# A cached-attention decode stack on one core: four edits at its first reads, its MLP weights, its last task and its last block

## The chip, the cores and the metric

The kernel runs on one core of one Trainium2 chip. The metric is device time in microseconds (us), the median of the runs of one program. A core has a matrix engine (PE, with its weight loads as PEld), VectorE (DVE), ScalarE (ACT), GpSimd (POOL), and SyncE (SP), which here only issues DMAs; 16 DMA engines move the data between HBM and SBUF. Each engine executes its own instructions in program order, and engines wait for one another through semaphores.

## The reference

```python
x = A_x                                                   # 8 sequences, 1 token each, D = 512
x = x + attention(layernorm(x), K, V, wq, wo)             # 32 query heads, 8 K/V heads, 8192 cached keys, Dh = 128
x = x + silu(layernorm(x) @ w1) @ w2                      # F = 1792
x = x + attention(layernorm(x), K, V, wq, wo)             # the same caches and weights again
x = x + silu(layernorm(x) @ w1) @ w2
# attention: q = x @ wq;  p = softmax(q K^T / sqrt(128));  o = p V;  o @ wo
# layernorm: (x - mean) / sqrt(var + 1e-5);   all tensors are bf16
```

K and V hold 134 MB each. Both layers read V whole; K is read in both layers except for 20 of the 32 granules of each sequence, which stay in SBUF between the layers. The HBM reads are 465 MB.

## The kernel before

**Tasks and positions.** A task is one (layer, sequence, K/V head); there are 128. A program loop counts positions p, eight to a task; each position emits the steps that are due on the engines. A granule is 512 KB of K or V, a quarter of one head's cache; it fills one of 28 slots of the SBUF tile ARENA. Per task: DVE transposes K in place (L485), PE forms the scores (L551) into PSUM bank SCp, DVE and POOL find the maximum (L562 to L574), ACT exponentiates (L578), PE and ACT transpose the probabilities (L596, L600), and PE multiplies them with V (`emit_pv`, L615), 14 positions (LP) behind the scores.

**A V product and its fold.** A V granule has 16 chunks of 128 keys per partition group. `emit_pv` takes four chunks at a time as 512 columns against 16 probability columns (4 chunks x 4 heads); of the result in the PSUM bank OTp only the blocks in which both chunks agree count. `emit_own` (ACT, L627) takes the first block of 128 columns with a mask (`own_x`), `emit_join` (DVE, L633, three instructions) adds the three others into the same f32 tile `joint`, `emit_fold` (PE, L640) sums the partitions in f32 with the mask `hm`, and `emit_norm` (DVE, L650) divides. All tasks do this alike. `add_heads` then applies wo to that head (L755).

**Loads.** SP issues every DMA, in program order (L376, or L102 where a separate wait precedes it). `plan_loads` fixes the order and the position after which each load's slot is free; `issue_until(p)` issues what is free after position p. At the start come x (8 rows), four K granules, wq, all loads that fit in the empty arena, then `load_rest`: wo in 1 KB rows, w1 in 3.5 KB rows, w2 in 1 KB rows (its rows dealt over partitions as ft*128 + p). After them come the loads that need a slot again. x lands in the tile E (also called P and Xr); PE transposes it with the identity matrix that POOL makes (L414, L417, L849), then comes the first LayerNorm and, when wq is there, the queries.

**Chains.** When a sequence has finished layer 0, its output projection, MLP and layer-1 queries are done one stage per position among the other tasks (`chain_of`). The first such chain starts at position 81.

**The last block.** After the last task the second MLP runs for all 8 sequences at once, with nothing beside it (`last_block`): residual add (L885), mean by a matmul with a constant matrix (L889), centring (`c32`, L894), squares and their sum (L897, L898), variance by an f32 matmul (L900), inverse root by Ln and Exp on ACT and a Newton step on DVE (L903 to L909, the result is `gain`), `xnT = c32 * gain` (L911), w1 in two halves of the hidden units (L919, 28 matmuls each, banks SCp 0 and 1), for each half the silu as exp (ACT, L924), add, reciprocal and product (DVE, L925 to L927, the result is `hsT`), w2 in two halves (L931), residual (L936), transposition (L942), two copies (L946, L948) and the store. `last_constants` (L879, L880) writes the constant matrices into an arena slot that is free by then, at the first position of the last task.

```python
def load_rest():
    dma(sp, wo_sb[:, :, :], A_wo.rearrange("(h p) d -> p h d", p=128), wsem["wo"], writes=["wo"])
    dma(sp, w1_sb[:, :, :], B_w1.rearrange("(kt p) f -> p kt f", p=128), wsem["w1"], writes=["w1"])
    dma(sp, w2_sb[:, :, :], B_w2.rearrange("(ft p) d -> p ft d", p=128), wsem["w2"], writes=["w2"])
```

Of the kernel before, what the change touches and what calls it, by code (L numbers as in the profile page):

```python
# [22 lines left out]
PRE = 10  # L23
LP = 14
EARLY = 4
WO_FROM = 36
NTP = 2
NSCP = 2
# [7 lines left out]
JOIN_AT = 1  # L36
FOLD_AT = 3
XW = 4
PIECES = (2, 2, 4)
NQS = 4  # L40
NAT = 2
CW = 32
SETTLE = 1
HALVES = 2

BF16 = mybir.dt.bfloat16
FP32 = mybir.dt.float32
# [193 lines left out]
def _build(ctx, nc, A_x, A_k_cache, A_v_cache, A_wq, A_wo, B_w1, B_w2, out):  # L241
# [120 lines left out]
    def op(eng, inst_fn, reads=(), writes=()):  # L362
        reads = [res(n) if isinstance(n, str) else n for n in reads]
        writes = [res(n) if isinstance(n, str) else n for n in writes]
        syn.acquire(eng, reads, writes)
        inst = inst_fn()
        tok = syn.mark(inst, eng)
        syn.release(tok, reads, writes)
        return tok

    def dma(eng, out_ap, in_ap, counter, reads=(), writes=()):
        reads = [res(n) if isinstance(n, str) else n for n in reads]
        writes = [res(n) if isinstance(n, str) else n for n in writes]
        syn.acquire(eng, reads, writes)
        tok = counter.next_tok()
        eng.dma_start(out_ap, in_ap).then_inc(counter.sem, 16)  # L376
        syn.release(tok, reads, writes)
        return tok

    def mm_group(steps, reads=(), writes=()):  # L380
        def run():
            inst = None
            for f in steps:
                inst = f()
            return inst
        return op(pe, run, reads, writes)
# [21 lines left out]
    with nc.Block() as block:  # L408

        @block.sync  # L410
        def _(sync_eng):
            dma(sp, Xr[0:B, :], x_in, wsem["x"], writes=["P"])

            op(pool, lambda: pool.memset(ident[:, :], 1.0), writes=["ident"])  # L414
            op(
                pool,
# [35 lines left out]
            def issue_until(pos):  # L452
                while queue and queue[0].after <= pos:
                    issue(queue.pop(0))
# [2 lines left out]
                dma(sp, wq_sb[:, :, :], A_wq.rearrange("(kt p) n -> p kt n", p=128), wsem["wq"], writes=["wq"])  # L457

            def load_rest():
                dma(sp, wo_sb[:, :, :], A_wo.rearrange("(h p) d -> p h d", p=128), wsem["wo"], writes=["wo"])  # L460
                dma(sp, w1_sb[:, :, :], B_w1.rearrange("(kt p) f -> p kt f", p=128), wsem["w1"], writes=["w1"])
                dma(sp, w2_sb[:, :, :], B_w2.rearrange("(ft p) d -> p ft d", p=128), wsem["w2"], writes=["w2"])

            for _n in range(NGRAN):
                issue(queue.pop(0))
            load_wq()
            issue_until(-2)
# [141 lines left out]
            def emit_pv(i):  # L609
                ti = i // GPT  # L610
                b, g, k, _h = where(i)
                slot = v_slot[(b, g, k)]
                ob, pb = ti % 2, ti % NPT
                steps = [
                    lambda t=t: pe.matmul(  # L615
                        OTp[ob][t * QUAD:t * QUAD + USED, :],
                        PT[pb][:, k, t].rearrange("p x r -> p (x r)"),
                        ARENA[:, slot * SLOT + t * KB:slot * SLOT + (t + 1) * KB],
                        start=(k == 0), stop=(k == NGRAN - 1),
                    )  # L620
                    for t in range(NQ)
                ]
                mm_group(steps, reads=[r_half(slot, 0), r_half(slot, 1), f"PT{pb}"], writes=[f"OT{ob}"])

            def emit_own(ti):
                ob = ti % 2
                op(act, lambda: act.activation(joint, OTp[ob][:, 0:DH], ACT.Copy, scale=own_x[:, 0:1]),  # L627
                   reads=[f"OT{ob}", "own_x"], writes=["P"])

            def emit_join(ti):  # L630
                ob = ti % 2
                for x in range(1, XW):
                    op(dve, lambda x=x: dve.scalar_tensor_tensor(  # L633
                        joint, OTp[ob][:, x * DH:(x + 1) * DH], own_x[:, x:x + 1], joint, op0=ALU.mult, op1=ALU.add),
                       reads=[f"OT{ob}", "own_x", "P"], writes=["P"])

            def emit_fold(ti):
                ob = ti % 2
                mm_group([
                    lambda: pe.matmul(OTp[ob][:, 0:REP], joint, hm[:, :], start=True, stop=True)  # L640
                ], reads=["P", "hm"], writes=[f"OT{ob}"])
# [231 lines left out]
            mean_w = spare[:, 0:128]  # L873
            words = spare[:, 128:].bitcast(FP32)
            var_w, c32, q32 = words[:, 0:128], words[:, 128:128 + KT * B], words[:, 160:160 + KT * B]
            part, gain, step_ = words[:, 192:192 + B], words[:, 200:200 + B], words[:, 208:208 + B]

            def last_constants():
                op(dve, lambda: dve.memset(mean_w, 1.0 / D), writes=r_calm + ["mean_w"])  # L879
                op(dve, lambda: dve.memset(var_w, 1.0 / D), reads=r_calm, writes=["var_w"])  # L880

            def last_block():

# [6 lines left out]
                    for k in range(KT)  # L890
# [3 lines left out]
                op(dve, lambda: dve.tensor_tensor(  # L894
                    c3, x1[:, :, :], QSp[:, 0:B].unsqueeze(1).to_broadcast(wide), ALU.subtract),
                   reads=["XT1", "QS"], writes=["c32"])
                op(dve, lambda: dve.tensor_tensor(q32, c32, c32, ALU.mult), reads=["c32"], writes=["q32"])  # L897
                op(dve, lambda: dve.tensor_reduce(part, q3.rearrange("p k b -> p b k"), AX.X, ALU.add),  # L898
                   reads=["q32"], writes=["part"])
                mm_group([lambda: pe.matmul(QSp[:, B:2 * B], var_w, part, start=True, stop=True)],  # L900
                         reads=["var_w", "part"], writes=["QS"])
                var = QSp[:, B:2 * B]
                op(act, lambda: act.activation(gain, var, ACT.Ln, bias=eps[:, 0:1], scale=GUESS ** -2),  # L903
                   reads=["QS", "eps"], writes=["gain"])
# [3 lines left out]
                   reads=["QS", "step_"], writes=["step_"])  # L908
                op(dve, lambda: dve.scalar_tensor_tensor(gain, step_, 3.0 * GUESS ** 2, gain, op0=ALU.subtract, op1=ALU.mult, reverse0=True),  # L909
                   reads=["step_", "gain"], writes=["gain"])  # L910
                op(dve, lambda: dve.tensor_tensor(xnT[:, :, :], c3, gain.unsqueeze(1).to_broadcast(wide), ALU.mult),  # L911
                   reads=["c32", "gain"], writes=["xnT"])

                cut = [FT * j // HALVES for j in range(HALVES + 1)]
                for j, (lo, hi) in enumerate(zip(cut, cut[1:])):
                    n = (hi - lo) * B
                    bank, rb = SCp[j % NSCP], f"SC{j % NSCP}"
                    mm_group([
                        lambda o=o, k=k: pe.matmul(bank[:, (o - lo) * B:(o - lo + 1) * B], w1_sb[:, k, o * 128:(o + 1) * 128], xnT[:, k, :],  # L919
                                                   start=(k == 0), stop=(k == KT - 1))  # L920
                        for o in range(lo, hi) for k in range(KT)
                    ], reads=["w1", "xnT"], writes=[rb])
                    ev, re = E[:, lo * B:hi * B], f"e_{j}"
                    op(act, lambda: act.activation(ev, bank[:, 0:n], ACT.Exp, scale=-1.0), reads=[rb, "P"], writes=[re])  # L924
                    op(dve, lambda: dve.tensor_scalar(ev, ev, 1.0, None, op0=ALU.add), reads=[re], writes=[re])  # L925
                    op(dve, lambda: dve.reciprocal(ev, ev), reads=[re], writes=[re])
                    op(dve, lambda: dve.tensor_tensor(hsT[:, lo * B:hi * B], bank[:, 0:n], ev, ALU.mult),  # L927
                       reads=[rb, re], writes=[f"hs_{j}"])
                for j, (lo, hi) in enumerate(zip(cut, cut[1:])):
                    mm_group([  # L930
                        lambda o=o, k=k: pe.matmul(  # L931
# [8 lines left out]
                for j in range(2):  # L940
# [7 lines left out]
                op(act, lambda: act.copy(Xr[0:B, w:D], SCp[1][0:B, 0:w]),  # L948
                   reads=["SC1"] + [f"e_{j}" for j in range(HALVES)], writes=["P2"])

            chain = []
            chain_b = [None]
            turn = [0]
            last0 = {b: max(task_at[(0, b, g)] for g in range(HKV)) for b in range(B)}
            first1 = {b: min(task_at[(1, b, g)] for g in range(HKV)) * GPT for b in range(B)}
            ntask = len(tasks)

            kept_from = min(g for g, _k in kept)

# [5 lines left out]
            for p in range(NG + LP + GPT + FOLD + 1):  # L965
# [32 lines left out]
                if done >= 0 and done % GPT == 0 and done // GPT < ntask:  # L998
                    tj = done // GPT
                    emit_norm(tj)  # L1000
                    layer, b, _g = tasks[tj]
                    if layer == 0:
                        heads[b].append(_g)
                    elif b == B - 1:
                        heads[B].append(_g)
                    if layer == 0 and tj == last0[b]:
                        assert not chain and turn[0] == b
                        chain.extend([lambda b=b: add_heads(b)] * (HKV - summed[b]) + chain_of(b))
                        chain_b[0] = b
                        turn[0] = b + 1  # L1010
                issue_until(p)
                if p == NG - GPT:
                    last_constants()
# [37 lines left out]
```

## Time and profile before

| | |
|---|---|
| median of 3 runs | 1164.85 us (1164.71 to 1164.93) |
| profiled execution | 1164.56 us |
| its span, first to last instruction | 1162.4 us |
| DVE, PE, ACT, POOL busy | 744.6, 730.0, 322.9, 116.7 us |
| PEld (beside PE) | 351.6 us |
| HBM read | 465.05 MB, 400 GB/s over the span |
| chain of waits, shares of the span | DMA 55%, SP's queue 15%, PE 12%, DVE 10% |

The page is of one profiled execution. Times within the span count from its first instruction. In a timeline line the columns are start, duration, engine, source line, operation, output and inputs, shapes, number of instructions merged, and in brackets how long the engine was idle before and what released it; "SPq" marks the issue of a DMA. In the windows, each line has a stretch of time, its length, busy time and number of instructions of PE, PEld, DVE, ACT and POOL, the granted PE clock, the mean share of the 16 DMA engines and GB/s.

### The profile page before, as it was taken

The page shows a single profiled execution, that of the slowest core. Times are in us where ns is not written, and L with a number is a line of the kernel's source. Part 1 is how long each engine was busy: PE and PEld are TensorE (multiplying, and loading weights), DVE is VectorE, ACT ScalarE, POOL GpSimd, SP SyncE. Part 2 cuts the span into 40 slices and gives each one's busy share as a digit, 9 for nine tenths or more (in the row PEclk, how much of TensorE's full clock was granted, in tenths as well). Part 3 has the DMA queues.
Part 4 walks back from the last instruction along what each step waited for, and adds up shares of the span by engine and source line. Part 5 has one row for each costly group of instructions (what it writes and reads, how often), then busy time and mean ns, then how long its engine had stood idle before and what let it go on. Part 6 is the DMA issues. An engine that isn't in the chain of part 4 may idle for free.

```text
span 1162.4 us, 27108 instructions
## 1 busy us (share of the span) xinstructions
PE 730.0 (63%) x11006; PEld 351.6 (30%) x11006; DVE 744.6 (64%) x1782; ACT 322.9 (28%) x759; POOL 116.7 (10%) x296
## 2 busy tenths in 40 slices
PE   1526677656765576567656676667666676657665
PEld 1212342223322342124222342234222332234233
DVE  3827674776557675767467755777477755767473
ACT  0203224223332233222422233222322232223322
POOL 0000101001110011001100011001100011001110
PEclk9995566555765566555855556555755576555655
DMA  9999999999999999999999999999999999999993
GB/s 369 394 397 411 408 408 414 416 410 402 404 418 413 409 402 417 414 409 402 413 414 413 404 394 416 416 409 407 409 417 411 407 403 419 412 408 403 409 408 159
DMA packets 116572, 466.84 MB, mean 402 GB/s; under 512 B 12240, under 2 KB 18144, under 8 KB 108768
## 3 DMA queue, kind: packets, MB, share of 16 engines
q1 hardware_dynamic: 116448, 465.11, 100.0%
q8 instruction: 87, 1.43, 0.5%
q14 instruction: 37, 0.30, 0.1%
HBM read 465.05 MB, written 0.01 MB: 400 GB/s over the span
## 4 chain that ended last, share of the span: by engine, by line
DMA 55%; SPq 15%; PE 12%; DVE 10%; issue 4%; ACT 3%; POOL 1%; DVEq 0%; ACTq 0%
DMA arena<-in_A_v_cache_dram 55%; SPq L376 15%; PE OTp L615 4%; DVE E L633 3%; DVE arena L485 2%; PE SCp L551 2%; PE MISC L737 2%; PE OTp L640 2%; PE TPp L596 1%; ACT E L578 1%; DVE row L562 1%; ACT PT L600 1%; POOL tops L567 1%; ACT E L627 1%; DVE row L574 1%
## 5 line engine op out<-in xcount | busy, mean ns | idle before, releaser
L485 DVE STREAM_TRANSPOSE arena<-arena 128x1024 int32<-128x1024 int32 x352 | 434.3, 1236 | 152.1 <-DMA arena<-in_A_k_cache_dram 151.7
L615 PE MATMUL OTp<-arena,PT 128*16 128x512 bf16 x2048 | 282.0, 553 | 295.7 <-DMA arena<-in_A_v_cache_dram 274.7
L578 ACT ACTIVATE E<-SCp,row 128x512 bf16<-128x512 f32 x128 | 181.9, 1421 | 596.0 <-DVE row L574 585.5
L551 PE MATMUL SCp<-arena,QB 128*16 128x128 bf16 (+2 forms) x4608 | 254.5, 366 | 20.5 <-DVE arena L485 14.0
L633 DVE SCALAR_TENSOR_TENSOR E<-OTp,row,E 128x128 f32<-128x128 f32 x384 | 131.4, 342 | 116.2 <-ACT E L627 105.0
L615 PEld LDWEIGHTS OTp<-arena,PT 128*16 128x16 bf16 x2048 | 50.3, 91 | 435.8 <-DMA arena<-in_A_v_cache_dram 401.1
L551 PEld LDWEIGHTS SCp<-arena,QB 128*16 128x16 bf16 x4608 | 107.3, 110 | 103.9 <-issue 52.5
L567 POOL PARTITION_ALL_REDUCE tops<-top x128 | 47.5, 371 | 582.2 <-DVE top L564 435.6
L596 PE MATMUL TPp<-ident,E 128*128 128x128 bf16 x512 | 71.7, 288 | 33.7 <-ACT E L578 32.6
L587 POOL PARTITION_ALL_REDUCE ssa<-ssm x128 | 55.8, 436 | 359.9 <-ACT ssm L585 359.9
L600 ACT COPY PT<-TPp 128x256 bf16<-128x256 bf16 x128 | 47.6, 372 | 156.1 <-PE TPp L596 156.1
L640 PE MATMUL OTp<-row,E 128*128 128x4 f32 x256 | 70.2, 345 | 24.4 <-DVE E L633 24.4
L562 DVE TENSOR_REDUCE row<-SCp 128x1 f32<-128x512 f32 x128 | 84.5, 660 | 0.7 <-PE SCp L551 0.7
L640 PEld LDWEIGHTS OTp<-row,E 128*128 128x128 f32 x256 | 59.0, 287 | 85.5 <-DVE E L633 49.9
L596 PEld LDWEIGHTS TPp<-ident,E 128*128 128x128 bf16 x512 | 40.8, 124 | 101.9 <-ACT E L578 72.0
L755 PE MATMUL MISC<-at,wo 128*128 128x32 bf16 x1024 | 37.3, 187 | 18.8 <-DVE row L571 12.7
L627 ACT ACTIVATE E<-OTp,row 128x128 f32<-128x128 f32 x128 | 47.5, 371 | 3.7 <-PE OTp L615 3.7
L737 PE MATMUL MISC<-xnT,wq 128*128 128x32 bf16 (+1 forms) x1152 | 35.6, 186 | 14.1 <-DVE xnT L724 14.1
L737 PEld LDWEIGHTS MISC<-xnT,wq 128*128 128x128 bf16 x1152 | 34.6, 105 | 20.6 <-issue 18.4
L755 PEld LDWEIGHTS MISC<-at,wo 128*128 128x128 bf16 x1024 | 32.9, 105 | 25.4 <-DVE at L650 22.3
L585 ACT ACTIVATE ssm<-row 128x4 f32<-128x4 f32 x128 | 37.9, 296 | 3.8
L525 DVE TENSOR_TENSOR QB<-QSp,row 128x64 bf16<-128x64 f32 x128 | 25.8, 202 | 19.6 <-PE QSp L512 19.5
(94 smaller groups left out, 302.6 us busy)
## 6 DMA issues: line engine op xcount, KB each, us to landing
arena<-in_A_v_cache_dram SPq DMA_DIRECT2D x512, 512.0 KB, 11.0
arena<-in_A_k_cache_dram SPq DMA_DIRECT2D x192, 512.0 KB, 8.3
arena<-in_A_k_cache_dram SPq DMA_DIRECT2D x24, 2048.0 KB, 22.3
arena<-in_A_k_cache_dram SPq DMA_DIRECT2D x32, 1024.0 KB, 19.9
wq<-in_A_wq_dram SPq DMA_DIRECT2D x1, 4096.0 KB, 16.5
wo<-in_A_wo_dram SPq DMA_DIRECT2D x1, 4096.0 KB, 35.0
w<-in_B_w_dram SPq DMA_DIRECT2D x2, 1792.0 KB, 26.5
E<-in_A_x_dram SPq DMA_DIRECT2D x1, 8.0 KB
```

The costliest lines, as they stand in the source:

```text
L376: eng.dma_start(out_ap, in_ap).then_inc(counter.sem, 16)
L485: op(dve, lambda: dve.transpose(words, words), reads=[r_half(slot, 0), r_half(slot, 1)], writes=[r_half(slot, 0), r_half(slot, 1)])
L551: lambda n=n, t=t: pe.matmul(SCp[bank][t * QUAD:t * QUAD + USED, lo * 128:(lo + len(slots)) * 128], QB[qn][:, n, :], keys(t, n), start=(n ...
L562: op(dve, lambda: dve.tensor_reduce(rowmax[:, :], SCp[bank][:, :], AX.X, ALU.max), reads=[f"SC{bank}"], writes=["rowmax"])
L578: op(act, lambda: act.activation(P[:, :].rearrange("p (x j k) -> p k x j", x=CPB, k=NGRAN), SCp[bank][:, :].rearrange("p (k x j) -> p k x ...
L596: lambda c=c: pe.transpose(tpv[:, c, :], P[:, c * 128:(c + 1) * 128], ident[:, :])
L600: op(act, lambda: act.copy(PT[pb][:, :, :, :, :].rearrange("p a t x r -> p x t a r"), tpv.rearrange("p x (t q) -> p x t q", q=QUAD)[:, :, ...
L615: lambda t=t: pe.matmul(OTp[ob][t * QUAD:t * QUAD + USED, :], PT[pb][:, k, t].rearrange("p x r -> p (x r)"), ARENA[:, slot * SLOT + t * KB ...
L633: op(dve, lambda x=x: dve.scalar_tensor_tensor(joint, OTp[ob][:, x * DH:(x + 1) * DH], own_x[:, x:x + 1], joint, op0=ALU.mult, op1=ALU.add ...
L640: lambda: pe.matmul(OTp[ob][:, 0:REP], joint, hm[:, :], start=True, stop=True)
L737: lambda o=o, k=k: pe.matmul(MISC[:, o * n:o * n + w], w_sb[:, k, o * 128:(o + 1) * 128], rhs_of(k).to_broadcast([128, w]) if n == 1 else ...
L755: lambda o=o, h=h: pe.matmul(MISC[:, o * w:(o + 1) * w], wo_sb[:, h, o * 128:(o + 1) * 128], rhs_of(h).to_broadcast([128, w]) if n == 1 el ...
```

## The change

Four edits:

1. The first K granule is issued ahead of x.
2. `load_rest` loads w1 first, into the memory of w2 (`undealt`), then wo. At the end of position 30, `deal_w1` has ACT copy w1 from there to its own place in four copies, one for each 128 input rows, with its columns reordered (hidden unit p*14 + ft goes to tile ft, place p), and SP then loads w2 in rows of 14 KB, partition p holding hidden units p*14 to p*14+13. The DMA of w2 waits for the four copies.
3. For the last task alone, each V granule is multiplied in two turns of 256 columns and 8 probability columns (XL = 2), both added into the same 256 columns of PSUM; ACT copies these 256 columns, and the fold is two f32 matmuls with the masks in `own_last` in place of the mask and the three additions. `last_constants` makes `own_last`.
4. In the last block w1 is applied to the centred rows (`xnT` is a copy of `c32`, on ACT) and its result scaled by `gain` (two DVE multiplications, into `scaled`). Two of the 14 column tiles of w1 (AHEAD) stand ahead of the variance matmul on PE, the others behind it. Both exponentials are emitted before the add, reciprocal and product of either half.

```diff
+DEAL_AT = 30
+XL = 2
+AHEAD = 2
...
-            dma(sp, Xr[0:B, :], x_in, wsem["x"], writes=["P"])
...
             def load_rest():
+                dma(sp, undealt, B_w1.rearrange("(kt p) f -> p kt f", p=128), wsem["w1"], writes=["w2"])
                 dma(sp, wo_sb[:, :, :], A_wo.rearrange("(h p) d -> p h d", p=128), wsem["wo"], writes=["wo"])
-                dma(sp, w1_sb[:, :, :], B_w1.rearrange("(kt p) f -> p kt f", p=128), wsem["w1"], writes=["w1"])
-                dma(sp, w2_sb[:, :, :], B_w2.rearrange("(ft p) d -> p ft d", p=128), wsem["w2"], writes=["w2"])
-
-            for _n in range(NGRAN):
+            undealt = w2_sb[:, :, :].rearrange("p ft d -> p (ft d)").rearrange("p (kt f) -> p kt f", kt=KT)
+            def deal_w1():
+                for k in range(KT):
+                    op(act, lambda k=k: act.copy(w1_sb[:, k, :].rearrange("p (ft q) -> p ft q", ft=FT),
+                                                 undealt[:, k, :].rearrange("p (q ft) -> p ft q", ft=FT)),
+                       reads=["w2"], writes=["w1"])
+                dma(sp, w2_sb[:, :, :], B_w2.rearrange("(p ft) d -> p ft d", p=128), wsem["w2"], writes=["w2"])
+            issue(queue.pop(0))
+            dma(sp, Xr[0:B, :], x_in, wsem["x"], writes=["P"])
+            for _n in range(1, NGRAN):
                 issue(queue.pop(0))
             load_wq()
             issue_until(-2)
             load_rest()
...
+                w = XL if ti == ntask - 1 else XW
                 steps = [
-                    lambda t=t: pe.matmul(
-                        OTp[ob][t * QUAD:t * QUAD + USED, :],
-                        PT[pb][:, k, t].rearrange("p x r -> p (x r)"),
-                        ARENA[:, slot * SLOT + t * KB:slot * SLOT + (t + 1) * KB],
-                        start=(k == 0), stop=(k == NGRAN - 1),
+                    lambda t=t, y=y: pe.matmul(
+                        OTp[ob][t * QUAD:t * QUAD + w * REP, 0:w * DH],
+                        PT[pb][:, k, t, y * w:(y + 1) * w].rearrange("p x r -> p (x r)"),
+                        ARENA[:, slot * SLOT + t * KB + y * w * DH:slot * SLOT + t * KB + (y + 1) * w * DH],
+                        start=(k == 0 and y == 0), stop=(k == NGRAN - 1 and y == CPB // w - 1),
                     )
-                    for t in range(NQ)
+                    for y in range(CPB // w) for t in range(NQ)
...
             def emit_own(ti):
+                if ti == ntask - 1:
+                    op(act, lambda: act.copy(E[:, 0:XL * DH], OTp[ob][:, 0:XL * DH]), reads=[f"OT{ob}"], writes=["P"])
+                    return
...
             def emit_join(ti):
+                if ti == ntask - 1:
+                    return
...
             def emit_fold(ti):
+                if ti == ntask - 1:
+                    mm_group([
+                        lambda x=x: pe.matmul(OTp[ob][:, 0:REP], E[:, x * DH:(x + 1) * DH], own_last[:, x * REP:(x + 1) * REP],
+                                              start=(x == 0), stop=(x == XL - 1))
+                        for x in range(XL)
+                    ], reads=["P", "own_last"], writes=[f"OT{ob}"])
+                    return
...
             def last_constants():
+                op(dve, lambda: dve.tensor_tensor(
+                    own_last.rearrange("p (x r) -> p x r", r=REP), own_x[:, 0:XL].unsqueeze(2).to_broadcast([128, XL, REP]),
+                    hm[:, :].unsqueeze(1).to_broadcast([128, XL, REP]), ALU.mult),
+                   reads=["own_x", "hm"] + r_calm, writes=["own_last"])
...
             def last_block():
+                op(act, lambda: act.copy(xnT[:, :, :], c3), reads=["c32"], writes=["xnT"])
                 op(dve, lambda: dve.tensor_tensor(q32, c32, c32, ALU.mult), reads=["c32"], writes=["q32"])
...
+                rise(0, AHEAD)
                 mm_group([lambda: pe.matmul(QSp[:, B:2 * B], var_w, part, start=True, stop=True)],
                          reads=["var_w", "part"], writes=["QS"])
+                rise(AHEAD, cut[1])
+                for lo, hi in zip(cut[1:], cut[2:]):
+                    rise(lo, hi)
...
-                op(dve, lambda: dve.tensor_tensor(xnT[:, :, :], c3, gain.unsqueeze(1).to_broadcast(wide), ALU.mult),
-                   reads=["c32", "gain"], writes=["xnT"])
...
+                    op(dve, lambda: dve.tensor_tensor(
+                        scaled[j].rearrange("p (o b) -> p o b", b=B), SCp[j][:, 0:n * B].rearrange("p (o b) -> p o b", b=B),
+                        gain.unsqueeze(1).to_broadcast([128, n, B]), ALU.mult),
+                       reads=[f"SC{j}", "gain"], writes=[f"scaled_{j}"])
...
+                if p == DEAL_AT:
+                    deal_w1()
                 issue_until(p)
```

`rise(lo, hi)` issues the w1 matmuls (four for each column tile) of the tiles lo to hi - 1.

More of the change, by code (lines that the diff above doesn't have):

```diff
@@ L459, in load_rest @@
             def load_rest():
+                dma(sp, undealt, B_w1.rearrange("(kt p) f -> p kt f", p=128), wsem["w1"], writes=["w2"])
                 dma(sp, wo_sb[:, :, :], A_wo.rearrange("(h p) d -> p h d", p=128), wsem["wo"], writes=["wo"])
-                dma(sp, w1_sb[:, :, :], B_w1.rearrange("(kt p) f -> p kt f", p=128), wsem["w1"], writes=["w1"])
-                dma(sp, w2_sb[:, :, :], B_w2.rearrange("(ft p) d -> p ft d", p=128), wsem["w2"], writes=["w2"])
-            for _n in range(NGRAN):
+            assert KT * F == FT * D
+            undealt = w2_sb[:, :, :].rearrange("p ft d -> p (ft d)").rearrange("p (kt f) -> p kt f", kt=KT)
[8 more added lines that the diff above has]
+            for _n in range(1, NGRAN):
                 issue(queue.pop(0))
@@ L875, in _ @@
             var_w, c32, q32 = words[:, 0:128], words[:, 128:128 + KT * B], words[:, 160:160 + KT * B]
+            own_last = words[:, 376:376 + XL * REP]
             part, gain, step_ = words[:, 192:192 + B], words[:, 200:200 + B], words[:, 208:208 + B]
@@ L899, in last_block, with rise @@
                    reads=["q32"], writes=["part"])
+                cut = [FT * j // HALVES for j in range(HALVES + 1)]
+                def rise(lo, hi):
+                    j = max(n for n in range(HALVES) if cut[n] <= lo)
+                    mm_group([
+                        lambda o=o, k=k: pe.matmul(SCp[j][:, (o - cut[j]) * B:(o - cut[j] + 1) * B],
+                                                   w1_sb[:, k, o * 128:(o + 1) * 128], xnT[:, k, :],
+                                                   start=(k == 0), stop=(k == KT - 1))
+                        for o in range(lo, hi) for k in range(KT)
+                    ], reads=["w1", "xnT"], writes=[f"SC{j}"])
+                assert HALVES <= NSCP
+                rise(0, AHEAD)
                 mm_group([lambda: pe.matmul(QSp[:, B:2 * B], var_w, part, start=True, stop=True)],
                          reads=["var_w", "part"], writes=["QS"])
+                rise(AHEAD, cut[1])
+                for lo, hi in zip(cut[1:], cut[2:]):
+                    rise(lo, hi)
                 var = QSp[:, B:2 * B]
@@ L910, in last_block @@
                    reads=["step_", "gain"], writes=["gain"])
-                op(dve, lambda: dve.tensor_tensor(xnT[:, :, :], c3, gain.unsqueeze(1).to_broadcast(wide), ALU.mult),
-                   reads=["c32", "gain"], writes=["xnT"])
-                cut = [FT * j // HALVES for j in range(HALVES + 1)]
+                scaled = [words[:, 256 + lo * B:256 + hi * B] for lo, hi in zip(cut, cut[1:])]
                 for j, (lo, hi) in enumerate(zip(cut, cut[1:])):
[L916 to L922, printed above, removed]
+                    n = hi - lo
+                    op(dve, lambda: dve.tensor_tensor(
+                        scaled[j].rearrange("p (o b) -> p o b", b=B), SCp[j][:, 0:n * B].rearrange("p (o b) -> p o b", b=B),
+                        gain.unsqueeze(1).to_broadcast([128, n, B]), ALU.mult),
+                       reads=[f"SC{j}", "gain"], writes=[f"scaled_{j}"])
                     ev, re = E[:, lo * B:hi * B], f"e_{j}"
-                    op(act, lambda: act.activation(ev, bank[:, 0:n], ACT.Exp, scale=-1.0), reads=[rb, "P"], writes=[re])
+                    op(act, lambda: act.activation(ev, scaled[j], ACT.Exp, scale=-1.0), reads=[f"scaled_{j}", "P"], writes=[re])
+                for j, (lo, hi) in enumerate(zip(cut, cut[1:])):
+                    ev, re = E[:, lo * B:hi * B], f"e_{j}"
                     op(dve, lambda: dve.tensor_scalar(ev, ev, 1.0, None, op0=ALU.add), reads=[re], writes=[re])
                     op(dve, lambda: dve.reciprocal(ev, ev), reads=[re], writes=[re])
-                    op(dve, lambda: dve.tensor_tensor(hsT[:, lo * B:hi * B], bank[:, 0:n], ev, ALU.mult),
-                       reads=[rb, re], writes=[f"hs_{j}"])
+                    op(dve, lambda: dve.tensor_tensor(hsT[:, lo * B:hi * B], scaled[j], ev, ALU.mult),
+                       reads=[f"scaled_{j}", re], writes=[f"hs_{j}"])
                 for j, (lo, hi) in enumerate(zip(cut, cut[1:])):
@@ L949, in last_block @@
                    reads=["SC1"] + [f"e_{j}" for j in range(HALVES)], writes=["P2"])
+            ntask = len(tasks)
             chain = []
@@ L955, in _ @@
             first1 = {b: min(task_at[(1, b, g)] for g in range(HKV)) * GPT for b in range(B)}
-            ntask = len(tasks)
             kept_from = min(g for g, _k in kept)
```

## The prediction
> **What bounds the kernel now.** I read the page's slices first, to see which resource is never idle.
>
> ```profile
> DMA  9999999999999999999999999999999999999993
> GB/s 369 394 397 411 408 408 414 416 410 402 404 418 413 409 402 417 414 409 402 413 414 413 404 394 416 416 409 407 409 417 411 407 403 419 412 408 403 409 408 159
> ```
>
> The DMA engines are full in every slice but the last. PE and DVE are busy under two thirds of the time, so work moved on them in the middle is worth nothing. The time is three pieces: the start of the stream, its bytes over its rate, and what is computed after the last bytes. Next I read the first issues in the timeline, and the rate by stretch in the windows (last column GB/s, the one before it the DMA share).
>
> ```profile
> 0.79 0.39 SPq L376 DMA_DIRECT2D E<-in_A_x_dram  x1
> 1.24 1.78 SPq L376 DMA_DIRECT2D arena<-in_A_k_cache_dram  x4
> ```
> ```profile
> 9.00:18.00 9.00, 0.24 (x4) 0.19 (x4) 2.93 (x12) 0.00 (x0) 0.28 (x1) 1.00 1.02 423
> 51.00:60.00 9.00, 0.64 (x8) 0.00 (x0) 4.06 (x8) 0.00 (x0) 0.37 (x1) 1.00 1.10 348
> 67.00:71.00 4.00, 0.00 (x0) 0.00 (x0) 0.00 (x0) 0.00 (x0) 0.00 (x0) 1.00 1.10 356
> 80.00:1140.00 1060.00, 694.02 (x10342) 330.02 (x10334) 699.68 (x1670) 308.29 (x727) 111.15 (x278) 0.58 1.02 410
> ```
>
> K's first transfer is issued 0.45 us after x. The stretches are wq in 8 KB rows (423), wo in 1 KB rows (348), w2 in 1 KB rows (356), and the caches, mostly 4 KB rows (410): 1 KB rows keep the engines just as busy and move a seventh less. Last comes the end: the chain of waits names the last transfer that anything waited for, and the timeline gives the steps behind it.
>
> ```profile
> 1121.70 15.49 DMA arena<-in_A_v_cache_dram
> ```
> ```profile
> 1148.63 0.37 ACT L627 ACTIVATE E<-OTp,row 128x128 f32<-128x128 f32 x1 [3.74 <-PE OTp L615]
> 1149.10 1.12 DVE L633 SCALAR_TENSOR_TENSOR E<-OTp,row,E 128x128 f32<-128x128 f32 x3 [2.14 <-ACT E L627]
> ...
> 1150.28 0.59 PE L640 MATMUL OTp<-row,E 128*128 128x4 f32 x2 [1.70 <-DVE E L633]
> ...
> 1152.38 0.19 DVE L894 TENSOR_TENSOR arena<-XT,QSp 128x32 f32<-128x32 bf16 x1 [0.43 <-PE QSp L889]
> ...
> 1153.10 0.59 PE L900 MATMUL QSp<-arena 128*128 128x8 f32 x2 [0.82 <-DVE arena L898]
> ...
> 1154.94 0.19 DVE L911 TENSOR_TENSOR xnT<-arena 128x32 bf16<-128x32 f32 x1
> ...
> 1155.19 1.66 PE L919 MATMUL SCp<-xnT,w 128*128 128x8 bf16 x56 [1.50 <-DVE xnT L911]
> ...
> 1156.39 0.19 DVE L925 TENSOR_SCALAR E<-E 128x56 f32<-128x56 f32 x1 [1.25 <-ACT E L924]
> ...
> 1158.18 0.22 DVE L927 TENSOR_TENSOR hsT<-SCp,E 128x56 bf16<-128x56 f32 x1
> ```
>
> The chain leaves the DMA at 1137.19 and is compute from there: softmax of the last task, its V product, fold, output projection, last block. The last V transfer is issued at 1132.4 and lands 14.9 later, at 1147.3, just ahead of the product that reads it. So whatever moves all landings earlier moves the end by as much, and the 14 us from there on are a chain in which every step counts.
>
> **The change, part by part.** The profiled execution is 1164.56 us, 1162.4 of span and 2.16 around it; the median of the runs is 1164.85. I work in differences and apply them to the median.
>
> *K first.* K's first issue moves from 1.24 to 0.79: the stream starts 0.45 us earlier. The second K issue stays at 1.65, while the first brings 512 KB, 1.28 us at 410 GB/s, and packets follow an issue by about a microsecond, so the stream doesn't run dry between. x now lands behind K's first granule, which took 3.9 from issue to landing, so at some 5 to 6 us. Its cover is the identity: the transposes of x (L849) wait for POOL's L417, done at 9.38; without that cover the first LayerNorm would start late, but the queries wait for wq at 19.5 anyway. Minus 0.45; bounds 0 and 0.45.
>
> *w2 in 14 KB rows.* 1.835 MB took 1.835/0.352 = 5.2 us at the 1 KB rates (348 and 356). At 410 to 423 they take 4.5 to 4.3. Minus 0.8; bounds 0.5 and 0.9. The page "DMA: Bandwidth & Descriptors" of the Trainium skill (Specifications) puts line rate at 512 B and up, by which 1 KB rows would be full rate already and this term nought; the rows at 348 and 356 say otherwise.
>
> *w1 landed in w2's place and dealt on ACT; w2 behind it.* w1 keeps its 3.5 KB rows, only ahead of wo. wo's issue lands 35.0 after 27.8, at 62.8; behind w1 it comes about 4 us later, 66.9, still ahead of its first use, which was at 77.0. The deal is four ACT copies of 1,792 elements with a read step of 28 bytes. Plain f32 or bf16 copies cost about 0.18 us plus 0.75 ns an element (128x32 0.18, 8x256 0.36), which makes 1.5 us each; the exponential L578, which writes in 8-byte steps, takes 1.42 us for 512, 2.4 ns an element, which makes 4.5. All four: 6 to 18 us. ACT stands idle from 50.1 to 76.9 in the trace of before, waiting for the exponential of task 3, and w1 lands at about 55: the deal ends between 61 and 73. The page "SBUF — State Buffer" (Door 1) of the Trainium skill says a step beyond 16 bytes pays for every access, which speaks for the upper figure. Either way it is hidden or delays the fourth exponential (71 now, since the V of task 2 no longer waits for w2) by 2 us, and the stream doesn't see that. The wait is new on SP's queue: w2 waits for the deal, and behind it stand all loads from position 37 on. By the loads' order, 15 loads (12 V granules and 4 MB of K, 10.5 MB, 25.6 us) lie between wo and w2, so they land by 66.9 + 25.6 = 92.5, and SP, which issues some 15 us ahead, comes to w2 at about 77. The deal is done by then. Cost 0.
>
> *The constants.* One more DVE multiply (0.2 to 0.36, as L525) at the place of L879; the PE waits over a microsecond for V at 1132 and 1137 behind it. Cost 0.
>
> *The last task.* Each of its four granules is 8 matmuls of 256 columns for 4 of 512. L551 runs 16 of 128 columns in the 0.60 us that L615 needs for 4 of 512: cost goes by columns. I take plus 0.05; the upper bound, if a matmul cost the same at 256, is a granule of 1.1 for 0.55, plus 1.7 in all, since the first two have 0.4 of slack before the fold of task 126. Then L627's 0.37 becomes a copy of 256 columns (0.36 by L948, 0.8 by L578's rate), the three L633 (1148.99 to 1150.28 with hops: 1.29) go, and the fold is two pairs of f32 passes: 0.59 plus about 0.50. Minus 1.29, plus 0.07 hop and 0.50: minus 0.7; bounds 0.3 and 0.8.
>
> *The last block.* Now c32 ends at 1152.57. After: ACT's copy to xnT 1152.62 to 1152.80; the first 8 matmuls of w1 (1.66/56 = 0.030 each) 1152.86 to 1153.10. Behind them in PE's queue stands the variance matmul, for which Ln, gain and both scalings wait; its input is ready at 1153.04, so it goes at 1153.12 for 1153.10. The gain is ready at 1154.94 for 1154.91. Meanwhile PE does the other 48, first half by 1154.4, second by 1155.2. The two scalings (0.22 each, as L927) run 1155.0 to 1155.5, the first exponential ends at 1155.51, and the six DVE operations that ran 1156.39 to 1158.40 start at 1155.56 and end at 1157.57. Minus 0.85; bounds 0.5 and 1.0. The w2 half behind it and the rest stay.
>
> Sum: -0.45 - 0.8 + 0.05 - 0.7 - 0.85 = -2.75 us: the profiled run 1161.8, the median 1162.1. A measurement of this kernel can tell about 0.2%, 2.3 us, from no change; the limit is 1162.5, so the forecast is faster by little over it.
>
> **Rivals.** *1 KB rows are no slower in this place:* the w2 term is nought, -1.95, 1162.9. For it: the engines' share was 1.10 in those stretches, so packets overlapped. Against it: two stretches at 350. 0.08. (The 512 B rule of the Trainium skill's DMA page would give this.)
>
> *The last engine.* The stream ends by its slowest DMA engine: in the windows its rate falls 406, 317, 180, 33 GB/s over 1140 to 1148, so engines end up to 4 us apart. Program fetches of 16 KB (87 of them) share these engines, 0.6 us each at 410/16 GB/s; two more on the last engine take 1.3 back: 1163.4. For it: the spread; against it: the program hardly grows. 0.13.
>
> *Matmuls cost by count,* the bound above: +1.7 for 0.05, 1163.75. L551 speaks against it. 0.06.
>
> *The deal holds SP* (the slower side). If the copies take so long that w2 is not issued by about 90, the stream runs dry, and each microsecond beyond is lost. To end 2.3 us slower it must eat 2.75 + 2.3 = 5.1 us, so end at 95: 40 us for four, 10 each, over twice what the slowest row gives. 1168 or so at 10.3 each. That, or a like stall of SP behind it: 0.06.
>
> **The numbers.** Forecast 0.67, rivals 0.08, 0.13, 0.06, 0.06. Faster by over 0.2%: 0.67; within 0.2%, the first three rivals: 0.27; slower: 0.06. The range runs from the good bounds of most terms, -0.45 - 0.9 - 0.8 - 1.0 = -3.15 with an engine's 0.8 more, 1160.9, up to the two middle rivals at 1163.5; it leaves out the deal's stall and the worst matmuls.
>
> **What would show it.** K's issue at 0.79; x after it, L849 still at 9.5. The stretch with w2 at 410 GB/s or more. Four ACT copies between 55 and 73, SP not waiting for them. The last V landing 1.25 earlier, at 1146.0. No L633 after it, four f32 passes in 1.1 us; the w1 matmuls beside Ln and gain, and hs of the second half done 2.75 us ahead of 1158.4. Wrong if SP waits for ACT near 77, if the last landing has not moved, or if the variance matmul starts over 0.3 us after its input.

## The result, and the profile after

The changed kernel takes 1162.26 us (median of 14 runs, 1161.62 to 1163.14); the kernel before takes 1164.64 us over the 14 runs beside them (1164.42 to 1164.93). The ratio is 0.9979, 95% interval 0.9971 to 0.9987: 2.4 us faster, and the interval leaves out no change. The runs of the changed kernel spread three times as far as those of before beside them, 1.5 us for 0.5; in the later series, with 26 to 33 runs, those of the kernel before spread by 1.4 to 1.6 too.

The profiled execution has a span of 1159.9 us, 2.5 less than before. Its end first, in the chain of waits (start, duration, what) and the timeline:

```profile
1121.35 15.10 DMA arena<-in_A_v_cache_dram
```
```profile
1147.91 0.37 ACT L641 COPY E<-OTp 128x256 f32<-128x256 f32 x1 [3.73 <-PE OTp L628]
...
1148.33 1.01 PE L659 MATMUL OTp<-arena,E 128*128 128x4 f32 x4 [0.48 <-ACT E L641]
...
1150.86 0.19 DVE L924 TENSOR_TENSOR arena<-XT,QSp 128x32 f32<-128x32 bf16 x1 [0.43 <-PE QSp L919]
1151.08 0.22 ACT L927 CAST xnT<-arena 128x32 bf16<-128x32 f32 x1 [2.80 <-DVE arena L924]
...
1151.35 0.38 PE L937 MATMUL SCp<-xnT,w 128*128 128x8 bf16 x8 [0.60 <-ACT xnT L927]
...
1151.59 0.57 PE L945 MATMUL QSp<-arena 128*128 128x8 f32 x2
...
1152.02 1.42 PE L937 MATMUL SCp<-xnT,w 128*128 128x8 bf16 x48
...
1153.49 0.34 DVE L962 TENSOR_TENSOR arena<-SCp,arena 128x56 f32<-128x56 f32 x2
...
1154.03 0.19 DVE L970 TENSOR_SCALAR E<-E 128x56 f32<-128x56 f32 x1 [0.19 <-ACT E L967]
...
1155.68 0.22 DVE L972 TENSOR_TENSOR hsT<-arena,E 128x56 bf16<-128x56 f32 x1
1156.89 0.19 DVE L981 TENSOR_TENSOR XT<-MISC,XT 128x32 bf16<-128x32 f32 x1 [1.00 <-PE MISC L976]
```

and the residual of the kernel before, to be read against the last of these lines:

```profile
1159.39 0.19 DVE L936 TENSOR_TENSOR XT<-MISC,XT 128x32 bf16<-128x32 f32 x1 [1.00 <-PE MISC L931]
```

These lines are read against the ones of before in three places. The transfer that the chain hangs on ends at 1136.45, where it was 1137.19: the stream gives 0.74. The centring (L924, before L894) starts at 1150.86 for 1152.38, 1.52 earlier: the last task gives 0.78 more. The last product of the silu (L972, before L927) starts at 1155.68 for 1158.18, 2.50 earlier: the block gives 0.98 more. The residual (L981, before L936) is 2.50 earlier as well, so the rest is unchanged. In the block one sees the w1 matmuls stand beside the variance, Ln and gain; they are done at 1153.44, before the scaling (L962) starts, and both its halves run without a wait between them.

So the two edits at the end gave a little more than forecast, and the stream 0.74 for a forecast 1.25. Where it fell short is seen at the start. The first lines are the timeline of the changed kernel; the windows after them (last column GB/s) are those of the changed kernel, and then of the kernel before.

```profile
0.79 0.39 SPq L379 DMA_DIRECT2D arena<-in_A_k_cache_dram  x1
1.24 0.36 SPq L379 DMA_DIRECT2D E<-in_A_x_dram  x1
1.65 1.29 SPq L379 DMA_DIRECT2D arena<-in_A_k_cache_dram  x3
```
```profile
1.50:3.50 2.00, 0.00 (x0) 0.00 (x0) 0.00 (x0) 0.56 (x1) 0.00 (x0) 1.00 0.77 190
3.50:5.50 2.00, 0.00 (x0) 0.00 (x0) 0.00 (x0) 0.00 (x0) 0.00 (x0) 1.00 0.95 317
5.50:7.50 2.00, 0.00 (x0) 0.00 (x0) 0.00 (x0) 0.00 (x0) 0.00 (x0) 1.00 0.95 350
7.50:9.50 2.00, 0.00 (x0) 0.00 (x0) 0.00 (x0) 0.00 (x0) 0.00 (x0) 1.00 1.04 389
```
```profile
1.50:3.50 2.00, 0.00 (x0) 0.00 (x0) 0.00 (x0) 0.57 (x1) 0.00 (x0) 1.00 0.58 137
3.50:5.50 2.00, 0.00 (x0) 0.00 (x0) 0.00 (x0) 0.00 (x0) 0.00 (x0) 1.00 0.96 350
5.50:7.50 2.00, 0.00 (x0) 0.00 (x0) 0.00 (x0) 0.00 (x0) 0.00 (x0) 1.00 1.00 393
7.50:9.50 2.00, 0.00 (x0) 0.00 (x1) 0.08 (x1) 0.00 (x0) 0.28 (x1) 1.00 1.08 434
```

K's stream does start earlier (190 for 137 GB/s in the first window), but the next three windows are each slower. Summed to 9.5 us the kernel before has brought 2.63 MB and the changed one 2.49: at 410 GB/s the lead of 0.45 us has become an arrears of 0.33. The size of this is rough, since traces of kernels with the same first loads differ: by 9.5 us the seven with x first brought 2.54 to 2.63 MB, the four with x second, the changed kernel among them, 2.30 to 2.50.

The second edit shows itself in ACT's timeline and in a window inside w2's transfer (93 to 95 us now):

```profile
55.64 13.61 ACT L469 COPY w<-w 128x1792 bf16<-128x1792 bf16 x4 [6.28 <-DMA w<-in_B_w_dram]
71.93 1.43 ACT L590 ACTIVATE E<-SCp,row 128x512 bf16<-128x512 f32 x1 [2.68 <-DVE row L586]
```
```profile
93.20:95.20 2.00, 1.84 (x24) 0.73 (x20) 0.00 (x0) 0.65 (x2) 0.00 (x0) 0.50 0.94 399
```

The deal takes 3.4 us a copy and ends at 69.25, before the exponential of task 3 is wanted; SP comes to w2 at 76.8, so nothing waits for the deal. w2 flows at 399 GB/s in this short window, for 356 before.

### The profile page after: what moved, and what is told of

It is laid out like the page before. It is cut to its first block, busy times and chain, and to the rows that moved or that the text cites. A ratio compares the mean times of both kernels' runs of the same rounds, so it can differ in the third digit from the quotient of the medians.

```text
span 1159.9 us, 27144 instructions
## 1 busy us (share of the span) xinstructions
PE 730.9 (63%) x11024; PEld 352.1 (30%) x11024; DVE 743.6 (64%) x1781; ACT 336.8 (29%) x764; POOL 116.8 (10%) x296
## 4 chain that ended last, share of the span: by engine, by line
DMA 56%; SPq 13%; PE 11%; DVE 11%; issue 4%; ACT 4%; POOL 1%; DVEq 0%; ACTq 0%
DMA arena<-in_A_v_cache_dram 51%; SPq L379 13%; DMA arena<-in_A_k_cache_dram 5%; PE OTp L628 4%; DVE arena L497 3%; DVE E L651 3%; PE SCp L563 2%; PE MISC L762 2%; PE TPp L608 2%; ACT E L590 2%; DVE row L574 1%; PE OTp L665 1%; ACT PT L612 1%; POOL tops L579 1%; DVE top L576 1%
## 5 line engine op out<-in xcount | busy, mean ns | idle before, releaser
L628 PE MATMUL OTp<-arena,PT 128*16 128x512 bf16 (+1 forms) x2064 | 283.1, 552 | 296.2 <-DMA arena<-in_A_v_cache_dram 275.5
L628 PEld LDWEIGHTS OTp<-arena,PT 128*16 128x16 bf16 (+1 forms) x2064 | 51.1, 91 | 436.7 <-DMA arena<-in_A_v_cache_dram 401.4
```

Of the source, the lines that this page charges most:

```text
L628: lambda t=t, y=y: pe.matmul(OTp[ob][t * QUAD:t * QUAD + w * REP, 0:w * DH], PT[pb][:, k, t, y * w:(y + 1) * w].rearrange("p x r -> p (x r)"),
```

## The experiments

Two theories stood against each other. **A**: the first edit is where the stream fell short, since K first costs more than its lead. **B**: K first is worth its 0.45, and the shortfall is an accident of one execution, or sits in the second edit. All times below are medians of 7 to 11 runs against the kernel before on the same chip, whose medians were 1164.76 to 1164.81; the intervals reach about 1 us to either side, so differences of half a microsecond are read from the traces.

**Each edit alone.** `e1_k_first` is the kernel before with

```diff
-            dma(sp, Xr[0:B, :], x_in, wsem["x"], writes=["P"])
...
+            issue(queue.pop(0))
+            dma(sp, Xr[0:B, :], x_in, wsem["x"], writes=["P"])
+            for _n in range(1, NGRAN):
```

> The kernel before with the first K granule ahead of x, nothing else. Theory A (the start is where the change falls short: K's first packets flow 0.45 us earlier, but the second to fourth granule are slower and the lead is gone by 10 us): 0 to +0.5 us against before, the fourth K granule landing at about 10.1 for 9.4. Rival B (the start is worth what the prediction says, and the changed kernel's slow start was one execution's accident): -0.45 us.

Measured: 1165.52 us, 0.76 slower, ratio 1.0005 (0.9996 to 1.0014); theory B's 0.45 faster would be 0.9996, at the interval's edge, and a loss is likely but not shown by these runs alone. Where the lead goes is clear in the trace. The time from issue to landing of the second granule, issued at 1.65, was 4.7 us in the kernel before and is here

```profile
L376 SPq DMA_DIRECT2D arena<-in_A_k_cache_dram x1: 344/344/344, 1.7 to 1.7; - x1
...
DMA to landing us min/median/max: 6.3/6.3/6.3
```

It was 5.7 in the changed kernel. The fourth granule lands at 10.5 us for 9.4. The traced execution is the fastest of its eleven, 1164.71 us: in it the transfer that the chain hangs on ends at 1137.20, for 1137.19 before. So the lead is gone at the end of the stream, and a loss beyond it does not show in this trace.

`e2_w2_rows` is the kernel before with the second edit (`undealt`, `deal_w1` at position 30, w2 in 14 KB rows).

> The kernel before with w1 landed first in the memory of w2, dealt on ACT, and w2 in 14 KB rows behind it, nothing else. Theory A: -1.0 us, by the landings of the changed kernel's trace (4.28 us for w2 where 5.26 stood). Rival B, in which the stream's missing half microsecond is lost here (the deal, or the place of w2): -0.3 us. The rule that 1 KB rows are full rate: 0.

Measured: 1163.92 us, 0.84 faster, ratio 0.9992 (0.9983 to 1.0001). The prediction's term was 0.8. Its window of 93.2 to 95.2 us has 406 GB/s. The transfer that the chain hangs on ends at 1136.25, for 1137.00 to 1137.56 in the five traces with x first and w2 in 1 KB rows (the kernel before, `e3_fold`, `e4_block`, `e7_w2_moved`, `e10_tail_only`).

`e3_fold` is the kernel before with the third edit, `e4_block` with the fourth.

> The kernel before with the last task's V product in turns of 256 columns, one copy and a two-step fold, nothing else. Both theories: -0.8 us by the changed kernel's trace (norm of the last task 1.53 earlier, of which 0.72 is the stream); the prediction had -0.65. If matmuls cost by count: +1.

> The kernel before with w1 on the centred rows and the scaling behind it, nothing else. Both theories: -0.97 us by the changed kernel's trace (the second half of hs 2.50 earlier, of which 1.52 lies ahead of the block); the prediction had -0.85.

Measured: 1164.05 us, 0.71 faster, ratio 0.9994 (0.9986 to 1.0003); and 1164.17 us, 0.59 faster, ratio 0.9993 (0.9984 to 1.0002). In their traces the time from the last V landing to the end of the span is 14.3 us (1147.3 to 1161.6) and 14.0 (1147.2 to 1161.2), for 15.1 before. Each edit shows in its own stretch: from the end of the chain's transfer to the centring `e3_fold` takes 14.39 us for 15.19, and from the centring to the residual `e4_block` takes 6.03 for 7.01. The runs of `e4_block` spread over 2.1 us, so its median says little; the two together were therefore run as `e10_tail_only`:

> The kernel before with the third and fourth edit together (last task and last block), the stream as before. Theory: the two add up, -1.75 us (by the changed kernel's trace -0.8 and -0.97; by the two parts' own medians -0.7 and -0.6, that is -1.3). Span minus last V landing 13.4 us for 15.1.

Measured: 1163.22 us, 1.59 faster, ratio 0.9985 (0.9977 to 0.9994), and 13.4 us from the last landing (1147.6) to the end (1161.0). The end gives 1.6 to 1.75 us; the prediction had 1.5.

**Where the second edit's gain is from.** `e7_w2_moved` keeps w2's later place, and leaves out the deal and the rows:

```diff
-                dma(sp, undealt, B_w1.rearrange("(kt p) f -> p kt f", p=128), wsem["w1"], writes=["w2"])
+                dma(sp, w1_sb[:, :, :], B_w1.rearrange("(kt p) f -> p kt f", p=128), wsem["w1"], writes=["w1"])
...
-                dma(sp, w2_sb[:, :, :], B_w2.rearrange("(p ft) d -> p ft d", p=128), wsem["w2"], writes=["w2"])
+                dma(sp, w2_sb[:, :, :], B_w2.rearrange("(ft p) d -> p ft d", p=128), wsem["w2"], writes=["w2"])
```

> The kernel before with w1 ahead of wo and w2 at position 30 as in the change, but w2 in 1 KB rows and w1 straight in its place, so no deal. Theory R (the gain of the second edit is the row size): 0 within 0.3 us of before, w2's stretch still near 350 GB/s. Rival P (it is the later place of w2): -0.8 us as the second edit alone.

Measured: 1164.80 us for 1164.76, ratio 1.0000 (0.9991 to 1.0009), and the same window inside w2's transfer reads

```profile
93.20:95.20 2.00, 1.68 (x24) 0.73 (x20) 0.00 (x0) 0.64 (x2) 0.00 (x0) 0.50 1.11 353
```

So the later place shows no gain of its own, and the gain goes with the rows: 353 GB/s in 1 KB rows and 399 to 406 in 14 KB rows, at the same place in the stream.

**Is the deal hidden?** `e8_deal_twice` doubles it in the changed kernel:

```diff
-                for k in range(KT):
+                for k in list(range(KT)) * 2:
```

> The changed kernel with the four deal copies executed twice over (the second pass writes the same values). The deal then ends at about 55.6 + 27.2 = 83 instead of 69 us, so SP waits some 5 us for it at 77. Prediction's cover (SP issues 15 us ahead of the landings): no change, -2.4 us against before. Rival (a hold of SP reaches the stream at once): +5 us, 2.5 us slower than before.

Measured: 1162.21 us, 2.55 faster than before, ratio 0.9978 (0.9969 to 0.9987): the changed kernel's own time. Here SP does wait, as ACT's timeline and the waits of SP's queue show (who waited for what: us in total, times, longest):

```profile
55.54 27.36 ACT L469 COPY w<-w 128x1792 bf16<-128x1792 bf16 x8 [4.38 <-DMA w<-in_B_w_dram]
82.80 1.38 ACT L590 ACTIVATE E<-SCp,row 128x512 bf16<-128x512 f32 x1
```
```profile
SPq L105 <- ACT w L469: 6.7, 1, 6.7
```

A hold of 6.7 us at SP, and an exponential some 11 us late, cost nothing that shows: what SP had issued ahead covered both. w2 is issued at 83.0 for 76.8, and lands at 97.2 us in both kernels (14.2 and 20.4 after its issue).

**What is wrong with K first.** Four kernels differ from the changed one only in where x is issued. `e5_x_first` puts it ahead of K again, `e11_x_third` behind two granules, `e6_x_fifth` behind all four, and `e12_x_act` gives it to ACT's queue while SP starts with K:

```diff
+            dma(act, Xr[0:B, :], x_in, wsem["x"], writes=["P"])
...
-            issue(queue.pop(0))
-            dma(sp, Xr[0:B, :], x_in, wsem["x"], writes=["P"])
-            for _n in range(1, NGRAN):
+            for _n in range(NGRAN):
```

> The changed kernel with x issued ahead of the first K granule again. Theory A (K first costs more than its 0.45 us lead brings, since the first packets of the stream are slow and x took that on itself while K was still being issued): 0.5 to 0.8 us faster than the changed kernel, so -2.9 to -3.2 us against before. Rival B (K first is worth its lead): 0.45 us slower than the changed kernel, so -2.0 us.

> The changed kernel with x issued behind all four K granules, ahead of wq. Theory A1 (x's eight packets between the first and second granule are what disturbs K): -2.9 us or better against before, the second K granule landing at 6 us again. Theory A2 (the first packets of the stream are slow whatever they carry, and with K first they are K's): no better than the changed kernel, -2.4 us, the second granule still late.

> The changed kernel with x issued behind two K granules. Theory A1a (a small transfer delays whatever granule comes right behind it while the stream starts up): the third granule lands late, over 8.5 us, and the time stays that of the changed kernel, -2.4 us against before. Theory A1b (only the place behind the very first transfer is bad): the granules land as with x behind all four, -3.0 us or better.

> The changed kernel with x issued by ACT on its own queue while SP issues the four K granules back to back. Theory Q (the delay comes from SP's queue, x standing between two granules there): the second K granule lands at about 6, -3.1 us against before. Theory E (it comes from the DMA engines taking a small transfer among K's first packets, whoever issues it): the second granule lands late again, -2.4 us.

Measured, with the landing of the second granule after its issue:

| | x stands | us | against before | ratio (95%) | second granule |
|---|---|---|---|---|---|
| `e8_deal_twice` | second | 1162.21 | -2.55 | 0.9978 (0.9969 to 0.9987) | 6.2 us |
| `e5_x_first` | first | 1161.83 | -2.93 | 0.9976 (0.9965 to 0.9986) | 4.8 us |
| `e11_x_third` | third | 1161.83 | -2.98 | 0.9975 (0.9965 to 0.9985) | 5.1 us |
| `e6_x_fifth` | fifth | 1161.57 | -3.19 | 0.9973 (0.9962 to 0.9983) | 4.6 us |
| `e12_x_act` | on ACT's queue | 1161.89 | -2.92 | 0.9974 (0.9964 to 0.9985) | 4.7 us |

The lines of the second granule in `e8_deal_twice` and in `e6_x_fifth`:

```profile
L379 SPq DMA_DIRECT2D arena<-in_A_k_cache_dram x1: 348/348/348, 1.7 to 1.7; - x1
...
DMA to landing us min/median/max: 6.2/6.2/6.2
```
```profile
L379 SPq DMA_DIRECT2D arena<-in_A_k_cache_dram x1: 420/420/420, 1.2 to 1.2; - x1
...
DMA to landing us min/median/max: 4.6/4.6/4.6
```

In all four kernels traced with x in second place (the changed one, `e1_k_first`, `e8_deal_twice`, `e9_ahead0`) the granule behind x takes 5.7 to 6.7 us; in the ten other traces the second granule takes 4.6 to 5.1. So theory A's place is right, but its reason is not: K first is not harmful in itself, since with x third, fifth or on ACT's queue the medians are as good as with x first. What goes with the late landing is x between the first granule and the second on SP's queue. Theory A2 falls with `e6_x_fifth`, and A1a with `e11_x_third`, whose third granule, issued at 2.1, lands after 5.9 us, for 6.0 in the kernel before.

Between Q and E `e12_x_act` does not decide. ACT issues x at the same moment as SP issues the first granule:

```profile
0.78 0.58 ACTq L379 DMA_DIRECT2D E<-in_A_x_dram  x1
```

The trace's packets of x have all started by 1.83 us, ahead of K's first; in the changed kernel they start between 3.6 and 4.3 us, among the first granules' packets. So here x was out of K's way in time as well as on another queue. Why a transfer of eight rows goes with this in that one place is not settled.

How much time it costs is known less well. The intervals of the times overlap, though the three kernels with x second have higher medians (1162.21 to 1162.91) than the four with x elsewhere (1161.57 to 1161.89). The transfer that the chain hangs on ends at 1136.45, 1136.81 and 1136.87 us in the traces with x second, at 1136.18 with x first and 1135.97 with x fifth; but also at 1136.62 with x third and 1136.58 with x on ACT's queue, whose second granules were not late. So a late second granule is not the whole of what sets the end of the stream.

**The order around the variance matmul.** `e9_ahead0` puts all w1 matmuls behind it:

```diff
-                rise(0, AHEAD)
...
-                rise(AHEAD, cut[1])
+                rise(0, cut[1])
```

> The changed kernel with all w1 matmuls behind the variance matmul (none ahead of it). By the changed kernel's trace the variance matmul goes 0.05 earlier and the second half of w1 ends 0.3 later, at which the second scaling waits 0.15: the end moves by -0.05 to +0.1 us, so -2.4 us against before. If the two tiles ahead were what hides w1 (rival), +0.3 us.

Measured: 1162.91 us, 1.90 faster than before, ratio 0.9982 (0.9973 to 0.9991), its runs 2.4 us apart; the median alone would be the rival's. The trace says otherwise. From the centring to the residual it takes

```profile
1151.29 0.19 DVE L924 TENSOR_TENSOR arena<-XT,QSp 128x32 f32<-128x32 bf16 x1 [0.43 <-PE QSp L919]
...
1157.32 0.19 DVE L980 TENSOR_TENSOR XT<-MISC,XT 128x32 bf16<-128x32 f32 x1 [1.00 <-PE MISC L975]
```

6.03 us, and in the changed kernel 1150.86 to 1156.89, also 6.03. The two tiles ahead buy nothing. What differs in this trace is the start: x is second here too, and the second granule took 6.7 us, the longest of all.

## Why the prediction was right

The forecast was 1162.1 and the time 1162.26. Its steps, one by one:

- *K first*, -0.45: this step failed. K's packets do flow earlier, but the prediction looked only at the issue times, and took it that the granules behind x would land as before. The trace shows the second granule 1.0 us later and three slower windows, and at the end of the stream no lead is left. In the medians the edit alone was 0.76 slower (the interval reaches from 0.5 faster to 1.6 slower), and taking it back from the changed kernel brought about 0.4, within the noise: no gain is shown, and a loss is likely. The worse of its two bounds was nought: a loss was excluded, and no reason given.
- *w2's rows*, -0.8: -0.84 alone, and the row size shown as its cause; the short windows have a little less than the 410 GB/s that was to be its sign. The Trainium skill's 512 B rule ("DMA: Bandwidth & Descriptors", Specifications) would have made it nought; the rates of 353 and 399 to 406 at one place speak against it here.
- *The deal*, nothing: right, with 3.4 us a copy inside the two bounds of 1.5 and 4.5, SP at w2 at 76.8 for a forecast 77, and the exponential of task 3 at 71.9 for 71. The doubled deal shows the cover. The 28-byte step costs more than a plain copy: 3.38 us for 1,792 elements, 1.8 ns an element beyond a fixed part of some 0.15 us, for 0.8 ns between the two plain copies that the prediction names (0.18 us for 32 elements, 0.36 for 256). With this the page "SBUF — State Buffer" (Door 1) of the Trainium skill agrees, by which an access that goes to a new 16-byte line pays a penalty.
- *The last task*, -0.65 with the product: -0.78 in the trace. The product's two granules took 1.02 us as before (1.03), with 16 matmuls of 256 columns in place of 8 of 512, so matmuls went by columns and that rival fell; the copy took 0.37 and the fold 1.01 for an estimate of 1.09.
- *The last block*, -0.85: -0.98. The variance matmul started by the forecast order; the term missed by the six DVE operations, 1.87 us (1154.03 to 1155.90) for 2.01. The operations are as long as before, but each product now starts 0.04 us after its reciprocal, for 0.10 and 0.11; that it reads DVE's own tile instead of PE's bank may be why, and is not tested.

Forecast -2.75; the terms that hold by the trace give -0.78 - 0.98 and, by the edit alone, -0.84, -2.6 in all, and the start took some of that back, which leaves the 2.38 measured. That the time came out within 0.16 us of the forecast is in part luck: the end was underrated by 0.26 where the start was overrated by some 0.65, and the kernel before took 1164.64 beside the change, 0.21 less than the 1164.85 from which the forecast counted. That the gain is over the 0.2% which the prediction set as its limit, 2.33 us of 1164.64, rests on 0.05 us.

## What to carry to other kernels

In this kernel, which a stream bounds, rows of 14 KB for rows of 1 KB brought about what the rates in the windows say, and 1 KB rows were as slow in the later place (353 GB/s) as in the earlier (356). The work on an idle engine that made this possible was free, since the issuing queue was far ahead: even a hold of 6.7 us did not show. An issue moved by half a microsecond at the start of the stream needs the landings behind it to be looked at, not only the issue times: `e6_x_fifth`, the changed kernel with x behind the four granules, has the lowest median of those run, 1161.57 us, by less than the noise. And where parts are worth half a microsecond each, the stretches of a trace in which they stand tell them apart better than medians that vary by one.

## What the runs showed of the hardware that was not expected

With an 8 KB transfer issued between the first and the second 512 KB transfer on SP's queue the second landed 5.7 to 6.7 us after its issue, in four traces, for 4.6 to 5.1 with the small one first, third, fifth or on ACT's queue; between the second and third it did not delay the third. And the stream ran below its later 410 GB/s up to 7.5 us: 137, 350 and 393 GB/s in the three windows from 1.5 on in the kernel before, 190, 317 and 350 in the changed one.
